# Attention decode: keys and values of both batch entries in one load of 32 KB rows, exponentials by batch entry

## The chip, the cores and the metric

One core of a Trainium2 chip. The metric is the device time of one execution in microseconds (us), without a profile for the comparison and with one for the traces. A kernel's time is the median of its runs; a verdict rests on ratios with a 95% interval. The batches of experiments ran on different chips, on which the kernel before took 190.50 to 190.68 us; times are therefore compared within a batch or by their ratios.

## The reference

One decode step: a layer norm of x (2 batch entries, 448 features), grouped-query attention with 16 query heads on 8 key/value heads over the last 4,096 cache positions, a dense layer with a Mish activation beside it, and the sum of x and both.

```python
W = min(4096, max(256, Sk // 4))                     # 4096 positions
q = (xn @ wq) -> (B, 16 heads, 256)
k = k_cache[:, :, Sk - W:, :]; v = v_cache[:, :, Sk - W:, :]   # 2 x 8 x 4096 x 256, bf16
p = softmax(q . k * 256 ** -0.5); o = p . v
out = x + o @ wo + (h * tanh(softplus(h))) @ w2      # h = xn @ w1 + b1
```

K and V are 67.1 MB of the 77.7 MB that one execution reads.

## The kernel before

It goes through 16 pairs of (key/value head, batch entry). Each pair's 4,096 keys lie as 128 partitions x 32 rows x 256 numbers, so that a partition's load is one run of 16 KB.

```python
heads = [(kvh, b) for kvh in range(Hkv) for b in range(Bsz)]
def load_k(i):                       # k_pool: 4 buffers of 16 KB a partition; V: 5
    kvh, b = heads[i]
    t = k_pool.tile([P, T * Dh], BF16, tag="k", name="k")
    nc.sync.dma_start(out=t[:],
        in_=A_k_cache[b, kvh, s0:Sk, :].rearrange("(p t) d -> p (t d)", p=P))
...
def turn(s):      nc.vector.transpose(kt, k half)        # 128 x 2048 words, L364
def scores(s):    8 matmuls of 512 columns into psc       # L376
                  nc.scalar.activation(out=p_sb, in_=psc, func=Exp, accum_out=rs)   # L386
def turn_p(s):    nc.vector.transpose(pT, p_sb)           # L397
def values(i):    16 matmuls of 512 columns, then 4 output transposes    # 12 of the pairs
def values_fixed(i):  64 matmuls of 2 columns, no transposes after it    # the last 4 pairs
def mix(kvh):     16 matmuls of 112 columns: oT @ wo into psA
...
for i in range(NK + KA):             # loads run two pairs ahead of the scores
    load_k(i + 2); load_v(i, cuts); load_wo(kvh)          # all on one DMA queue, in this order
    for half in range(NH): turn(s + 1); scores(s); turn_p(s - 1); close(i - KA - 1)
    build_q(i + 2); values(i - KA)
```

The last V load is cut into 1 MB, 0.5 MB and 0.5 MB, and the last weights come after it.

The softmax here doesn't subtract the row's maximum and nothing guards it: scores larger than these inputs give would overflow.

## Time and profile before

| | before |
|---|---|
| time, median of 3 | 190.59 us (190.53 to 190.59) |
| span of the profiled run | 188.7 us |
| packets of the big DMA queue, MB | 7,796, 77.66 |
| mean rate over the span | 413 GB/s, 428 to 431 in the middle |
| busy: TensorE, VectorE, ScalarE | 76%, 60%, 17% |

A busy share says little here; what counts is that the row of DMA digits has no hole. The lines are in the prediction below.

### The profile page before, as it was taken

The numbers are of one execution on the slowest core, as the hardware profiler recorded it, in microseconds if no ns is written. First come the engines' busy times: TensorE is split into PE (matmuls) and PEld (weight loads), VectorE is DVE, ScalarE is ACT, GpSimd is POOL, SyncE is SP. The second block draws the span as 40 slices with busy tenths as digits, with TensorE's granted clock in tenths as the row PEclk, the third lists the DMA queues.
The fourth block names the chain that finished last, engine by engine and source line by source line (L and its number), as shares of the span: only waits on it lengthen the run. The fifth ranks groups of instructions, "written<-read, shape, count | busy, mean of one in ns | idle before, by whom it ended". The sixth has DMA issues, their size and how long they took to land.

```text
span 188.7 us, 2944 instructions
## 1 busy us (share of the span) xinstructions
PE 144.1 (76%) x1158; PEld 71.7 (38%) x1158; DVE 113.5 (60%) x195; ACT 32.5 (17%) x82; POOL 27.1 (14%) x139
## 2 busy tenths in 40 slices
PE   0152991788995799869985999769986999597782
PEld 0042390234442345334432434324533443254671
DVE  7805505997919392857649381939376673939401
ACT  2300110112212022111222112202311121211101
POOL 8004430033030022003030203003110300000000
PEclk9999995799999699988999699969998799969955
DMA  6999999999999999999999999999999999999991
GB/s 216 423 432 422 430 430 434 438 431 420 417 441 431 420 416 438 441 427 405 442 434 429 434 420 431 434 431 420 431 431 438 412 432 434 431 441 417 408 394 49
DMA packets 7816, 77.86 MB, mean 413 GB/s; under 512 B 757, under 2 KB 2809, under 8 KB 3322
## 3 DMA queue, kind: packets, MB, share of 16 engines
q1 hardware_dynamic: 7796, 77.66, 97.3%
q8 instruction: 9, 0.15, 0.3%
q14 instruction: 5, 0.04, 0.1%
q10 hardware_dynamic: 6, 0.01, 0.0%
HBM read 77.67 MB, written 0.00 MB: 412 GB/s over the span
## 4 chain that ended last, share of the span: by engine, by line
DMA 82%; DVE 11%; issue 2%; PE 2%; SPq 1%; ACT 0%; ACTq 0%
DMA k<-in_A_k_cache_dram 68%; DMA v<-in_A_v_cache_dram 14%; DVE kt L364 8%; DVE pT L397 2%; PE sc L376 1%; SPq L114 0%; PE psA L214 0%; SPq L338 0%; PE q L479 0%; SPq L280 0%; DVE sums L407 0%; SPq L275 0%; DVE sums L404 0%; DVE den_sb L320 0%; ACT p L386 0%
## 5 line engine op out<-in xcount | busy, mean ns | idle before, releaser
L364 DVE STREAM_TRANSPOSE kt<-k 128x2048 f32<-128x2048 f32 x32 | 73.4, 2296 | 50.6 <-DMA k<-in_A_k_cache_dram 49.6
L376 PE MATMUL sc<-kt,qdiag 128*128 128x512 bf16 x256 | 72.7, 433 | 17.6 <-DVE kt L364 15.8
L376 PEld LDWEIGHTS <-qdiag 128*128 128x128 bf16 x256 | 24.7, 105 | 57.2 <-issue 30.0
L431 PE MATMUL o<-v,pT 128*4 128x512 bf16 x192 | 43.4, 379 | 0.0
L264 POOL COPY qdiag<-qrep 32x8 bf16<-32x8 bf16 x128 | 23.1, 213 | 122.4 <-PE sc L376 107.6
L386 ACT ACTIVATE p<-sc 128x512 bf16<-128x512 f32 x32 | 19.1, 597 | 95.6 <-PE sc L376 93.1
L431 PEld LDWEIGHTS <-pT 128*4 128x4 bf16 x192 | 15.8, 87 | 21.8
L397 DVE STREAM_TRANSPOSE pT<-p 128x512 bf16<-128x512 bf16 x32 | 21.5, 672 | 1.1 <-ACT p L386 1.1
L439 ACT COPY o_sb<-o 4x512 f32<-4x512 f32 x12 | 6.9, 574 | 36.8 <-PE o L431 36.8
L214 PE MATMUL psA<-wo,oT 128*2 128x112 bf16 x128 | 3.8, 245 | 11.0 <-DVE oT L447 11.0
L479 PE MATMUL q<-pT,v 128*128 128x2 bf16 x256 | 7.6, 165 | 1.7 <-DMA v<-in_A_v_cache_dram 1.6
L460 PEld LDWEIGHTS q<-ident_f,o_sb 4*128 4x128 f32 x48 | 6.6, 206 | 5.1 <-issue 5.1
L479 PEld LDWEIGHTS <-v 128*128 128x128 bf16 x256 | 7.3, 101 | 2.0 <-DMA v<-in_A_v_cache_dram 2.0
L414 PEld LDWEIGHTS den<-sums,ones_f 128*128 128x128 f32 x32 | 6.8, 220 | 3.3 <-issue 1.7
L460 PE MATMUL q<-ident_f,o_sb 4*128 4x4 f32 x48 | 7.6, 261 | 0.0
L235 PE MATMUL qT_ps<-xs,v 128*128 128x4 bf16 x112 | 3.3, 166 | 4.8 <-DVE ones L201 2.8
L214 PEld LDWEIGHTS <-oT 128*2 128x2 bf16 x128 | 1.8, 87 | 11.9 <-DVE oT L447 11.7
L386 ACT ACTIVATION_READ_ACCUMULATOR p<-sc 128x1 f32 x32 | 6.2, 194 | 0.0
L177 PE MATMUL xnT_ps<-ident,xn_bf 2*128 2x2 bf16 x7 | 0.5, 167 | 6.3 <-DVE xn_bf L139 6.3
L414 PE MATMUL den<-sums,ones_f 128*128 128x2 f32 x32 | 5.1, 229 | 0.0
L235 PEld LDWEIGHTS <-v 128*128 128x128 bf16 x112 | 3.1, 104 | 5.0 <-issue 3.0
L462 DVE COPY osum<-q 128x4 f32<-128x4 f32 x12 | 1.9, 158 | 3.9 <-PE q L460 3.9
(52 smaller groups left out, 46.5 us busy)
## 6 DMA issues: line engine op xcount, KB each, us to landing
k<-in_A_k_cache_dram SPq DMA_DIRECT2D x16, 2048.0 KB, 31.5
v<-in_A_v_cache_dram SPq DMA_DIRECT2D x15, 2048.0 KB, 34.8
v<-in_B_w_dram SPq DMA_DIRECT2D x2, 1568.0 KB, 21.0
wo<-in_A_wo_dram SPq DMA_DIRECT2D x7, 448.0 KB, 31.5
v<-in_A_wq_dram SPq DMA_DIRECT2D x1, 2048.0 KB
v<-in_A_wq_dram SPq DMA_DIRECT2D x1, 1536.0 KB, 10.8
v<-in_A_v_cache_dram SPq DMA_DIRECT2D x1, 1024.0 KB, 29.1
v<-in_A_v_cache_dram SPq DMA_DIRECT2D x2, 512.0 KB, 27.4
```

What stands on the lines that cost most here:

```text
L214: nc.tensor.matmul(part(n), lhsT=lhsT, rhs=w[:, n * DO : (n + 1) * DO], start=start, stop=stop, tile_position=(0, n * Q), skip_group_check ...
L235: nc.tensor.matmul(qT_ps[:, hh, e, :], lhsT=wq_v[s][:, hh, e, :], rhs=xs[:, s, :, :].rearrange("p x b -> p (x b)"), start=(s == 0), stop=( ...
L264: nc.gpsimd.tensor_copy(out=tv[rows, :, e, j * Q : (j + 1) * Q : HS], in_=qrep[rows, :, h0 : h0 + rep, e, x, b],)
L364: nc.vector.transpose(out=kt[:].bitcast(FP32), in_=k[:, half * TH * Dh : (half + 1) * TH * Dh].bitcast(FP32),)
L376: nc.tensor.matmul(psc[:], lhsT=qdiag[i % NW][:, n * NE + e, :], rhs=ktv[:, n, e, :, :], start=(n == 0 and e == 0), stop=(n == NB - 1 and ...
L386: nc.scalar.activation(out=p_sb[:], in_=psc[:].rearrange("p t c -> p (t c)"), func=ACT.Exp, scale=scale, accum_out=state["rs", i][:, s % N ...
L397: nc.vector.transpose(out=pT[:], in_=p_t.pop(s)[:])
L414: nc.tensor.matmul(den[:], lhsT=ones_f[:], rhs=state.pop(("sums", i))[:], start=True, stop=True)
L431: nc.tensor.matmul(po[:], lhsT=pT_t[i * NH + half][:, uh * NP * Q : (uh + 1) * NP * Q : HS], rhs=v[:, u * NP : (u + 1) * NP, :].rearrange( ...
L439: nc.scalar.copy(out=o_sb[:], in_=po[:])
L460: nc.tensor.transpose(pqv[:, u, c, :], ov[:, u, c, :], ident_f[0:NR, 0:NR])
L479: nc.tensor.matmul(po[:, c, :], lhsT=vv[:, t, c, :], rhs=pTv[:, th, 0:Q:HS], start=(t == 0 and c == 0), stop=(t == T - 1), skip_group_chec ...
```

## The change

The intent: read both batch entries of a head at once, so that loads are 4 MB and rows 32 KB, and halve the number of loads, denominators and output transposes. Partition 2p + b holds row p of entry b. A score row belongs to one entry, so the exponentials of the other entry's partitions must vanish: two exponentials over every second column, with a bias of 0 on the rows of their own entry and -10,000 on the others.

```diff
-    T = W // P
-    NH = 2
+    PB = P // Bsz
+    T = W // PB
+    TH = 16
+    NH = T // TH
...
-    k_pool = ... bufs=4
-    v_pool = ... bufs=5
+    k_pool = ... bufs=2          # of twice the size
+    v_pool = ... bufs=2
...
+    def load_cache(t, cache, i, cuts):
+        src = cache[:, i, s0:Sk, :].rearrange("b (p t) d -> p b (t d)", p=PB)
+        for lo, hi in zip(cuts, cuts[1:]):
+            cols = slice(lo * Dh, hi * Dh)
+            nc.sync.dma_start(out=t[:, cols], in_=src[:, :, cols])
...
-        nc.scalar.activation(out=p_sb[:], in_=psc[:]..., func=ACT.Exp, scale=scale, accum_out=...)
+        for b in range(Bsz):
+            nc.scalar.activation(out=pv[:, b, :, :], in_=sv[:, b, :, :], func=ACT.Exp,
+                scale=scale, bias=off[:, b : b + 1], accum_out=...)
...
-            load_v(i, (0, T) if i < NK - 1 else (0, T // 2, 3 * T // 4, T))
+            load_v(i, (0, T) if i < Hkv - 1 else (0, T // 2, 7 * T // 8, T))
...                                # query building, output transposes and sums by head, not by pair
```

The last V load is now cut into 2 MB, 1.5 MB and 0.5 MB.

More of the change, by code (lines that the diff above doesn't have):

```diff
@@ L61 @@
     F = B_w1.shape[1]
-    T = W // P
-    NH = 2
-    TH = T // NH
+    PB = P // Bsz
+    T = W // PB
+    TH = 16
+    NH = T // TH
+    BR = Bsz * rep
     NX = 2
@@ L73 @@
     NE = 2
-    HS = Q // rep
+    HS = Q // BR
     assert Sq == 1 and D * NX == NS * P and NS % 2 == 1 and HF % P == 0 and Hq % NX == 0
@@ L83 @@
     wo_pool = ctx.enter_context(tc.tile_pool(name="wo", bufs=3))
-    k_pool = ctx.enter_context(tc.tile_pool(name="kk", bufs=4))
-    v_pool = ctx.enter_context(tc.tile_pool(name="vv", bufs=5))
-    kt_pool = ctx.enter_context(tc.tile_pool(name="kt", bufs=3))
+    k_pool = ctx.enter_context(tc.tile_pool(name="kk", bufs=2))
+    v_pool = ctx.enter_context(tc.tile_pool(name="vv", bufs=2))
+    kt_pool = ctx.enter_context(tc.tile_pool(name="kt", bufs=4))
     consts = ctx.enter_context(tc.tile_pool(name="consts", bufs=1))
@@ L100, with v_tile @@
     nc.scalar.dma_start(out=b1_sb[:, :], in_=B_b1.rearrange("(o f) -> o f", o=1))
-    def v_tile(n):
-        t = v_pool.tile([P, T * Dh], BF16, tag="v", name="v")
-        return t[:, 0:n]
-    SC = NS // 2 + 1
-    wq_in = A_wq.rearrange("r (x n) -> (r x) n", x=NX).rearrange("(p s) n -> p s n", s=NS)
-    wq_sb = []
-    for lo, hi in ((0, SC), (SC, NS)):
-        w = v_tile((hi - lo) * HW).rearrange("p (s n) -> p s n", n=HW)
-        nc.sync.dma_start(out=w, in_=wq_in[:, lo:hi, :])
-        wq_sb += [w[:, s, :] for s in range(hi - lo)]
+    def v_tile():
+        return v_pool.tile([P, T * Dh], BF16, tag="v", name="v")
+    wq_sb = v_tile()[:, 0 : NS * HW].rearrange("p (s n) -> p s n", s=NS)
+    nc.sync.dma_start(
+        out=wq_sb,
+        in_=A_wq.rearrange("r (x n) -> (r x) n", x=NX).rearrange("(p s) n -> p s n", s=NS),
+    )
     make_identity(nc, ident[:])
@@ L158 @@
             )
-    hsel = hsel[:, 0:rep]
+    hsel = hsel[:, 0:BR]
     nc.vector.tensor_copy(out=hsel, in_=ident[:, 0:Q:HS])
@@ L164 @@
         )
+    off = consts.tile([P, Bsz], FP32)
+    for b in range(Bsz):
+        nc.vector.tensor_reduce(
+            out=off[:, b : b + 1], in_=hsel[:, b * rep : (b + 1) * rep], axis=AXIS.X, op=ALU.add
+        )
+    mine = consts.tile([P, 1], FP32)
+    nc.vector.tensor_reduce(out=mine[:], in_=hsel, axis=AXIS.X, op=ALU.add)
+    nc.vector.tensor_scalar(
+        out=off[:], in0=off[:], scalar1=mine[:], scalar2=1e4, op0=ALU.subtract, op1=ALU.mult
+    )
     ones_f = consts.tile([P, P], FP32)
     nc.gpsimd.memset(ones_f[:], 1.0)
-    NW = 3
+    NW = 2
     qdiag = []
@@ L227 @@
     qrep = consts.tile([P, NB, HH, NE, NX, Bsz], BF16)
-    wq_v = [w.rearrange("p (h m e) -> p h e m", h=HH, e=NE) for w in wq_sb]
+    wq_v = wq_sb.rearrange("p s (h m e) -> p s h e m", h=HH, e=NE)
     def project():
@@ L236, in project @@
                         qT_ps[:, hh, e, :],
-                        lhsT=wq_v[s][:, hh, e, :],
+                        lhsT=wq_v[:, s, hh, e, :],
                         rhs=xs[:, s, :, :].rearrange("p x b -> p (x b)"),
@@ L252, in project @@
         )
-    heads = [(kvh, b) for kvh in range(Hkv) for b in range(Bsz)]
     def build_q(i):
-        kvh, b = heads[i]
-        x, h0 = divmod(kvh * rep, HH)
+        x, h0 = divmod(i * rep, HH)
         t = qdiag[i % NW]
@@ L264, in build_q @@
                 nc.gpsimd.tensor_copy(
-                    out=tv[rows, :, e, j * Q : (j + 1) * Q : HS],
-                    in_=qrep[rows, :, h0 : h0 + rep, e, x, b],
+                    out=tv[rows, :, e, j * Q : (j + 1) * Q : HS].rearrange(
+                        "p n (b h) -> p n b h", b=Bsz
+                    ),
+                    in_=qrep[rows, :, h0 : h0 + rep, e, x, :].rearrange("p n h b -> p n b h"),
                 )
@@ L273, in load_dense @@
     def load_dense():
-        dense["w1"] = v_tile(NS * HF).rearrange("p (s n) -> p s n", s=NS)
+        w = v_tile()
+        dense["w1"] = w[:, 0 : NS * HF].rearrange("p (s n) -> p s n", s=NS)
         nc.sync.dma_start(
@@ L278, in load_dense @@
         )
-        dense["w2"] = v_tile(NX * NF * D).rearrange("p (x c d) -> p x c d", x=NX, c=NF)
+        dense["w2"] = w[:, NS * HF : NS * HF + NX * NF * D].rearrange(
+            "p (x c d) -> p x c d", x=NX, c=NF
+        )
         nc.sync.dma_start(
@@ L328, in dense_out, with load_k @@
                 add(act_bf[:, c, x, :], w2_sb[:, x, c, :])
-    NSTEP = len(heads) * NH
+    NSTEP = Hkv * NH
     k_t, kt_t, v_t, p_t, pT_t, wo_t = {}, {}, {}, {}, {}, {}
     state = {}
-    def load_k(i):
-        kvh, b = heads[i]
-        t = k_pool.tile([P, T * Dh], BF16, tag="k", name="k")
-        nc.sync.dma_start(
-            out=t[:], in_=A_k_cache[b, kvh, s0:Sk, :].rearrange("(p t) d -> p (t d)", p=P)
-        )
-        k_t[i] = t
-    def load_v(i, cuts=(0, T)):
-        kvh, b = heads[i]
-        t = v_tile(T * Dh).rearrange("p (t d) -> p t d", t=T)
-        vin = A_v_cache[b, kvh, s0:Sk, :].rearrange("(p t) d -> p t d", p=P)
-        for lo, hi in zip(cuts, cuts[1:]):
-            nc.sync.dma_start(out=t[:, lo:hi, :], in_=vin[:, lo:hi, :])
-        v_t[i] = t
+    def load_cache(t, cache, i, cuts):
[3 more added lines that the diff above has]
+            nc.sync.dma_start(out=t[:, cols], in_=src[:, :, cols])
+    def load_k(i, cuts=(0, T)):
+        k_t[i] = k_pool.tile([P, T * Dh], BF16, tag="k", name="k")
+        load_cache(k_t[i], A_k_cache, i, cuts)
+    def load_v(i, cuts=(0, T)):
+        t = v_tile()
+        load_cache(t, A_v_cache, i, cuts)
+        v_t[i] = t[:].rearrange("p (t d) -> p t d", t=T)
     def load_wo(kvh, parts=1):
@@ L383, in scores @@
         p_sb = p_pool.tile([P, TH * Q], BF16, tag="p", name="p")
-        if s % NH == 0:
-            state["rs", i] = small.tile([P, NH], FP32, tag="rs", name="rs")
-        nc.scalar.activation(
-            out=p_sb[:],
-            in_=psc[:].rearrange("p t c -> p (t c)"),
-            func=ACT.Exp,
-            scale=scale,
-            accum_out=state["rs", i][:, s % NH : s % NH + 1],
-        )
+        piece = s % NH
+        if piece == 0:
+            state["rs", i] = small.tile([P, NH, Bsz], FP32, tag="rs", name="rs")
+        pv = p_sb[:].rearrange("p (t c b) -> p b t c", t=TH, b=Bsz)
+        sv = psc[:].rearrange("p t (c b) -> p b t c", b=Bsz)
+        for b in range(Bsz):
+            nc.scalar.activation(
+                out=pv[:, b, :, :],
+                in_=sv[:, b, :, :],
+                func=ACT.Exp,
+                scale=scale,
+                bias=off[:, b : b + 1],
+                accum_out=state["rs", i][:, piece, b : b + 1],
+            )
         p_t[s] = p_sb
     def turn_p(s):
-        pT = p_pool.tile([P, TH * Q], BF16, tag="pT", name="pT", bufs=7)
+        pT = p_pool.tile([P, TH * Q], BF16, tag="pT", name="pT", bufs=2 * NH + 1)
         nc.vector.transpose(out=pT[:], in_=p_t.pop(s)[:])
@@ L402, in turn_p @@
         rs = state.pop(("rs", i))
-        sums = small.tile([P, rep], FP32, tag="sums", name="sums", bufs=4)
+        total = small.tile([P, 1], FP32, tag="total", name="total")
+        nc.vector.tensor_reduce(out=total[:], in_=rs[:], axis=AXIS.XY, op=ALU.add)
+        sums = small.tile([P, BR], FP32, tag="sums", name="sums")
         nc.vector.tensor_scalar(
-            out=sums[:], in0=hsel, scalar1=rs[:, 0:1], scalar2=None, op0=ALU.mult
-        )
-        nc.vector.scalar_tensor_tensor(
-            out=sums[:], in0=hsel, scalar=rs[:, 1:2], in1=sums[:], op0=ALU.mult, op1=ALU.add
+            out=sums[:], in0=hsel, scalar1=total[:], scalar2=None, op0=ALU.mult
         )
@@ L412, in denominator @@
     def denominator(i):
-        den = ps_m.tile([P, rep], FP32, tag="m", name="den")
+        den = ps_m.tile([P, BR], FP32, tag="m", name="den")
         nc.tensor.matmul(
@@ L416, in denominator @@
         )
-        rec = small.tile([P, rep], FP32, tag="rec", name="rec")
+        rec = small.tile([P, BR], FP32, tag="rec", name="rec")
         nc.vector.reciprocal(out=rec[:], in_=den[:])
@@ L421 @@
     NP = 2
-    NR = NP * rep
+    NR = NP * BR
     def values(i):
@@ L429, in values @@
         for u in range(T // NP):
-            half, uh = divmod(u, TH // NP)
+            piece, uh = divmod(u, TH // NP)
             nc.tensor.matmul(
                 po[:],
-                lhsT=pT_t[i * NH + half][:, uh * NP * Q : (uh + 1) * NP * Q : HS],
+                lhsT=pT_t[i * NH + piece][:, uh * NP * Q : (uh + 1) * NP * Q : HS],
                 rhs=v[:, u * NP : (u + 1) * NP, :].rearrange("p t d -> p (t d)"),
@@ L442, in scale_o @@
     def scale_o(i, o):
-        kvh, b = heads[i]
         rec = state.pop(("rec", i))
-        if b == 0:
-            state["oT"] = small.tile([P, ND, rep, Bsz], BF16, tag="oT", name="oT")
+        oT = small.tile([P, ND, rep, Bsz], BF16, tag="oT", name="oT")
         nc.vector.tensor_tensor(
-            out=state["oT"][:, :, :, b],
-            in0=o,
-            in1=rec[:].unsqueeze(1).to_broadcast([P, ND, rep]),
+            out=oT[:].rearrange("p c h b -> p c b h"),
+            in0=o.rearrange("p c (b h) -> p c b h", b=Bsz),
+            in1=rec[:]
+            .rearrange("p (b h) -> p b h", b=Bsz)
+            .unsqueeze(1)
+            .to_broadcast([P, ND, Bsz, rep]),
             op=ALU.mult,
         )
+        state["oT", i] = oT
     def finish(i):
@@ L460, in finish @@
                 nc.tensor.transpose(pqv[:, u, c, :], ov[:, u, c, :], ident_f[0:NR, 0:NR])
-        o = small.tile([P, ND, rep], FP32, tag="osum", name="osum")
-        nc.vector.tensor_copy(out=o[:], in_=pqv[:, 0, :, 0:rep])
+        o = small.tile([P, ND, BR], FP32, tag="osum", name="osum")
+        nc.vector.tensor_copy(out=o[:], in_=pqv[:, 0, :, 0:BR])
         for u in range(1, NP):
             nc.vector.tensor_tensor(
-                out=o[:], in0=o[:], in1=pqv[:, u, :, u * rep : (u + 1) * rep], op=ALU.add
+                out=o[:], in0=o[:], in1=pqv[:, u, :, u * BR : (u + 1) * BR], op=ALU.add
             )
-        scale_o(i, o[:])
+        scale_o(i, o)
     def values_fixed(i):
@@ L472, in values_fixed @@
         pq = ps_q.tile([P, NP * ND * NR], FP32, tag="q", name="q")
-        po = pq[:, 0 : ND * rep].rearrange("p (c h) -> p c h", c=ND)
+        po = pq[:, 0 : ND * BR].rearrange("p (c h) -> p c h", c=ND)
         vv = v_t.pop(i).rearrange("p t (m c) -> p t c m", c=ND)
         for t in range(T):
-            half, th = divmod(t, TH)
-            pTv = pT_t[i * NH + half][:].rearrange("p (t c) -> p t c", t=TH)
+            piece, th = divmod(t, TH)
+            pTv = pT_t[i * NH + piece][:].rearrange("p (t c) -> p t c", t=TH)
             for c in range(ND):
@@ L489, in mix @@
     def mix(kvh):
-        oT = state["oT"]
+        oT = state.pop(("oT", kvh))
         w = wo_t.pop(kvh)
@@ L498, in mix, with close @@
                 )
-    NK = len(heads)
-    KA = 2
+    NFIX = 2
+    def close(i):
+        if i < Hkv - NFIX:
+            finish(i)
+        mix(i)
     load_k(0)
     load_dense()
-    load_k(1)
     project()
@@ L509 @@
     turn(0)
-    NFIX = 4
-    def close(i):
-        if i < NK - NFIX:
-            finish(i)
-        kvh, b = heads[i]
-        if b == Bsz - 1:
-            mix(kvh)
-    for i in range(NK + KA):
-        if i + 2 < NK:
-            load_k(i + 2)
-        if i < NK:
-            load_v(i, (0, T) if i < NK - 1 else (0, T // 2, 3 * T // 4, T))
-            kvh, b = heads[i]
-            if b == Bsz - 1:
-                load_wo(kvh, parts=1 if i < NK - 1 else 2)
-            for half in range(NH):
-                s = i * NH + half
+    for i in range(Hkv + 1):
+        if i + 1 < Hkv:
+            load_k(i + 1, (0, T) if i + 1 < Hkv - 1 else (0, T // 2, T))
+        if i < Hkv:
+            load_v(i, (0, T) if i < Hkv - 1 else (0, T // 2, 7 * T // 8, T))
+            load_wo(i, parts=1 if i < Hkv - 1 else 2)
+            for piece in range(NH):
+                s = i * NH + piece
                 if s + 1 < NSTEP:
@@ L535 @@
                     turn_p(s)
-                if half == 0 and i > KA:
-                    close(i - KA - 1)
-            if i + 2 < NK:
+                if piece == 0 and i > 1:
+                    close(i - 2)
+            if i + 2 < Hkv:
                 build_q(i + 2)
-        if i == NK:
-            close(i - KA - 1)
+        else:
+            close(i - 2)
         if i == 0:
             dense_in()
-        if i == 1:
             dense_out()
-        if i >= KA:
-            if i - KA < NK - NFIX:
-                values(i - KA)
-            else:
-                values_fixed(i - KA)
-        if i >= NK:
-            close(i - KA)
+        if i >= 1:
+            if i - 1 < Hkv - NFIX:
+                values(i - 1)
+            else:
+                values_fixed(i - 1)
+        if i == Hkv:
+            close(i - 1)
     res = consts.tile([Bsz, D], BF16)
```

## The prediction

The forecast is 190.59 - 1.0 = 189.6 us: 0.9 us for packets and 0.14 us for completions, both from packet times in the trace of the kernel before, and 0 for all else. The completions are the 754 packets of 4 bytes in the trace of the kernel before, 16 for each of 47 loads and 2 more, with a median of 9 ns.

> **What bounds the kernel now.** I read the page from its slices to its chain of waits, then the windows view, the groups and the timeline of the end. The slices come first, because they tell whether one resource is busy throughout:
>
> ```profile
> PE   0152991788995799869985999769986999597782
> DVE  7805505997919392857649381939376673939401
> PEclk9999995799999699988999699969998799969955
> DMA  6999999999999999999999999999999999999991
> GB/s 216 423 432 422 430 430 434 438 431 420 417 441 431 420 416 438 441 427 405 442 434 429 434 420 431 434 431 420 431 431 438 412 432 434 431 441 417 408 394 49
> ```
>
> The reader is to see that the DMA row is 9 from the second slice to the last but one, while PE and DVE come and go. The kernel streams 77.66 MB and computes in the shadow of it. The chain of waits and the queue table say the same in shares:
>
> ```profile
> q1 hardware_dynamic: 7796, 77.66, 97.3%
> ...
> DMA 82%; DVE 11%; issue 2%; PE 2%; SPq 1%; ACT 0%; ACTq 0%
> DMA k<-in_A_k_cache_dram 68%; DMA v<-in_A_v_cache_dram 14%; DVE kt L364 8%; DVE pT L397 2%; PE sc L376 1%; SPq L114 0%; PE psA L214 0%; SPq L338 0%; PE q L479 0%; SPq L280 0%; DVE sums L407 0%; SPq L275 0%; DVE sums L404 0%; DVE den_sb L320
> ```
>
> Packets of the one big queue fill 97.3% of 16 engines for the whole span: 183.6 of 188.7 us. The DVE share of the chain is no second bound: a buffer's release is one of the events before an issue, but the queue in front of that issue is still full, as the windows show (us, busy of PE, weight load, DVE, ACT, POOL, then clock, DMA share, GB/s):
>
> ```profile
> 40.00:60.00 20.00, 17.23 (x80) 7.38 (x80) 14.76 (x20) 3.90 (x10) 3.45 (x20) 1.00 1.01 428
> ...
> 120.00:140.00 20.00, 17.89 (x92) 7.82 (x92) 12.53 (x20) 3.61 (x10) 2.91 (x16) 0.91 1.01 431
> ```
>
> DMA share is 1.01 in every middle window. What remains outside the stream is the start (the first packet starts at 1.7 us) and the end: the last V packets end at 183.9 us, the last value matmuls run from 184.31, the output is issued at 186.51, and the span ends at 188.7. That is 1.7 + 4.8 us around a stream of 182 us. The groups I need for costs:
>
> ```profile
> L364 DVE STREAM_TRANSPOSE kt<-k 128x2048 f32<-128x2048 f32 x32 | 73.4, 2296 | 50.6 <-DMA k<-in_A_k_cache_dram 49.6
> L376 PE MATMUL sc<-kt,qdiag 128*128 128x512 bf16 x256 | 72.7, 433 | 17.6 <-DVE kt L364 15.8
> L431 PE MATMUL o<-v,pT 128*4 128x512 bf16 x192 | 43.4, 379 | 0.0
> L386 ACT ACTIVATE p<-sc 128x512 bf16<-128x512 f32 x32 | 19.1, 597 | 95.6 <-PE sc L376 93.1
> L397 DVE STREAM_TRANSPOSE pT<-p 128x512 bf16<-128x512 bf16 x32 | 21.5, 672 | 1.1 <-ACT p L386 1.1
> L386 ACT ACTIVATION_READ_ACCUMULATOR p<-sc 128x1 f32 x32 | 6.2, 194 | 0.0
> ```
>
> DVE's idle time (49.6 us) is mostly a wait for K to land: the engines wait for the data, not the data for them.
>
> [...] Built, the new load reads a pattern of 64 x 2 x 16384 elements into 128 partitions[...]. No load of the kernel before has unequal outer sizes, so its trace shows nothing of this. [...]
>
> **The change part by part.**
> *Loads.* Sixteen K loads and as many V heads of 2 MB become eight of 4 MB each, with rows of 32 KB where there were 16 KB. The bytes are the same. In the packet records of the trace, grouped by size, a packet is one row: medians are 74 ns for 1,792 bytes, 159 for 4,096, 309 for 8,192, 460 for 12,288 and 611 for 16,384. From 8,192 to 16,384 bytes, (611 - 309)/8192 = 0.0369 ns a byte, and 309 - 302 = 7 ns that do not scale. So I estimate 1,215 ns for a 32 KB packet, against 2 x 611. Count: before, 31 whole loads and 3 pieces of 128 rows are 4,352 packets; after, 14 whole loads, 2 pieces of K and 3 of V are 19 x 128 = 2,432. The query weights, now one load, save another 128. Saved: 2,048 packets x 7 ns / 16 engines = 0.9 us. Each load also writes one completion of 9 ns an engine: 48 loads of that queue become 32, 16 x 9 ns = 0.14 us. All on the path, since the stream is the bound: **-1.0 us**.
> *TensorE and VectorE.* Counted in the built programs: scores stay 256 matmuls of 512 columns, values 192 of 512 and 256 small ones (4 columns for 2), transposes 32 + 32. Denominators go from 16 to 8, output transposes from 48 to 24, and their small VectorE operations halve: together they are busy for 15.2 us now, so some 7.6 us go, all of it beside the stream: **0**.
> *ScalarE.* 32 exponentials of 512 become 64 of 256 with a pointer bias. [...] PT is needed only a head later: **0**.
> *GpSimd.* 128 query copies become 64 of twice the width, in the shadow: **0**.
> *Buffers.* K has 2 of 32 KB a partition instead of 4 of 16, V 2 instead of 5 halves. A head is now 4.19 + 4.19 + 0.46 MB, at 430 GB/s 9.8 + 9.8 + 1.05 = 20.6 us. Take K(i) landed at 0. Its four transposes with four of P between them last 4 x (2.30 + 0.67) = 11.9 us, then its buffer is free. The transfer that needs it, K(i+2), starts after V(i-1), weights, K(i+1), V(i), weights: at 31.4 us. Slack 19 us. V(i-1) is free after the scores (about 14 us) and 32 value matmuls of 43.4/192 = 0.226 us, 7.2 us: at 21 us; V(i+1) starts at 41 us. Even with scores at the slow clock (the timeline has one group of 8 in 3.32 us instead of 1.90), 13 us are left. **0**.
> *Start.* The second buffer of V first holds both dense weights, and V(1) must wait for the dense product, which VectorE does behind the transpose of K(1). K(1) lands near 15.3 MB / 0.43 = 36 + 2 us; the product is done near 45 us; V(1)'s turn in the queue is near 57. **0**.
> *End.* The last V piece is 512 KB as before (8 of 64 rows a partition for 8 of 32), followed by the same weights, 16 value matmuls and 16 matmuls of the output: **0**, with 0.3 us either way.
>
> Sum: 190.59 - 1.0 = 189.6 us.
>
> **Rivals.** *A, the deal of rows to engines or the two distant entries slow the stream.* Neighbouring rows now lie 128 MiB apart in HBM[...]. For it: nothing in the trace has this pattern. Against it: [...] each row is long, and the order within partitions is plain. A mild form (1 to 2% lower rate) gives 191 to 193 us[...]. I give the two together 10%. *B, two coarse buffers open gaps in the stream.* For it: PE is busy 17 to 18 of every 20 us, so a head needs nearly its whole period, and arrivals are lumpier. Against: the slack of 13 to 20 us above. One gap of 2 us at the start would make 191.5; one a head would make over 200. I give 5%. *C, the longer rows buy more than 7 ns.* [...] 5%.
>
> **Range and chances.** The mechanism gives -1.0 with an uncertainty of some 0.7 for the fit of the 7 ns and the end. A mild form of A or B stretches the range upwards. Range 188.6 to 191.3. Faster by over 2% (under 186.8) needs C and more: 0.04. Slower by over 2% (over 194.4) needs A or B in full: 0.09. Within 2%: 0.87.
>
> **What would show it right or wrong.** Right: the DMA row stays at 9, about 5,490 packets in the big queue (7,796 - 2,048 - 256), packets of 32 KB near 1,215 ns, middle windows at 431 to 434 GB/s[...], the last load to the end unchanged at 4 to 5 us. Wrong: 32 KB packets over 1,230 ns or GB/s below 425 with the DMA row at 9 speak for A; a digit under 9 in the middle of the DMA row, with the queue waiting for a transpose or a value matmul, speaks for B; GB/s over 435 for C.

## The result

| | before | after |
|---|---|---|
| median of 4 runs each | 190.56 us (190.51 to 190.59) | 190.46 us (190.30 to 190.64) |
| ratio of the means | | 0.9995, interval 0.9978 to 1.0013 |

Ratios are the mean time of one kernel's fast runs over that of the other's from the same rounds, so they are not quite the ratio of the medians quoted. The time lies inside the predicted range, but the forecast gain of 1.0 us did not come: 0.1 us did, no more than noise, and a repetition (below) had 0.0.

The page of the changed kernel, the lines that answer to those shown of before (DMA share and rate in 40 slices, queues, chain of waits):

```profile
DMA  6999899999999999999999999999999999999990
GB/s 226 445 444 428 383 432 438 445 442 440 431 431 438 445 407 404 433 438 398 462 447 431 431 431 438 414 418 420 449 431 431 412 423 435 473 418 386 427 375 23
...
q1 hardware_dynamic: 5492, 77.66, 96.8%
q8 instruction: 8, 0.13, 0.2%
...
DMA 67%; DVE 18%; PE 11%; ACT 1%; SPq 0%; issue 0%; ACTq 0%; DVEq 0%
```

The packets fell by 2,304, as counted. Queue q8, of kind "instruction", moves packets of 16 KB (8 of them, 0.13 MB), called fetches below. They seem to be TensorE's: the runs with 11 matmuls alone, stream32 and stream16, have none, and 1,152 more TensorE instructions (more_instr) come with four more, 12 for 8. One digit in the early part is an 8. It is no gap: the packet records show at least 16 packets in flight at every moment from 12 to 172 us, read here as all 16 engines busy, and the run with loads alone (below) has the same 8. Two of the six middle windows, and the groups of the exponentials (all six, from 40 to 160 us, run at 422 to 435 GB/s, 429.7 on average, against 428.7 before):

```profile
40.00:60.00 20.00, 14.91 (x115) 6.97 (x116) 12.62 (x16) 4.52 (x17) 1.64 (x8) 0.81 1.02 435
...
120.00:140.00 20.00, 16.52 (x83) 6.87 (x81) 12.15 (x14) 4.87 (x17) 1.64 (x8) 0.83 1.00 428
```

```profile
L403 ACT ACTIVATE p<-sc,off 128x256 bf16<-128x256 f32 x64 | 33.0, 544 | 84.2 <-PE sc L389 83.5
...
L403 ACT ACTIVATION_READ_ACCUMULATOR p<-sc,off 128x1 f32 x64 | 11.7, 183 | 0.0
```

ScalarE's share rose from 17% to 22%, in the shadow. What the DMA queue's issues waited for (total us, times, longest), before and then after:

```profile
SPq L348 <- DMA k<-in_A_k_cache_dram: 31.3, 7, 4.5
```

```profile
SPq L353 <- PE o L448: 55.0, 6, 11.4
SPq L353 <- DVE kt L377: 54.3, 6, 10.3
```

The new kernel's issues do wait for value matmuls and transposes, 109 us in all, because it has two buffers. Yet the stream has no hole: a K load is issued a median of 29.7 us before it lands, so these waits are inside the slack. The rival of coarse buffers is out.

**The last microseconds** differ. The windows of 1 us (same columns as above; the last two are DMA share and GB/s), before:

```profile
182.00:183.00 1.00, 0.88 (x32) 0.79 (x30) 0.00 (x0) 0.00 (x0) 0.00 (x0) 0.50 1.00 406
183.00:184.00 1.00, 0.59 (x16) 0.51 (x16) 0.00 (x0) 0.00 (x0) 0.00 (x0) 0.50 0.89 350
184.00:185.00 1.00, 0.59 (x16) 0.50 (x16) 0.07 (x1) 0.00 (x0) 0.00 (x0) 0.50 0.59 219
```

and after:

```profile
182.00:183.00 1.00, 0.25 (x9) 0.25 (x10) 0.00 (x0) 0.00 (x0) 0.00 (x0) 0.50 0.93 360
183.00:184.00 1.00, 1.00 (x43) 1.00 (x41) 0.00 (x0) 0.00 (x0) 0.00 (x0) 0.50 0.55 213
184.00:185.00 1.00, 0.74 (x29) 0.63 (x25) 0.17 (x1) 0.00 (x0) 0.00 (x0) 0.50 0.12 43
```

From 183 us on, most engines of the new kernel have nothing left (share 0.55, then 0.12, against 0.89 and 0.59). The trace records 16 landings for the last V piece, taken here as one for each of the 16 DMA engines: the first at 182.55 and the last at 184.27 us before, at 181.79 and 183.95 after. Before, the matmuls that read the piece begin at 184.31, just after the last. Most engines are done earlier by most of the gain that was forecast, but some work on: the first engine gained 0.76 us, the last 0.32.

The timeline after that piece (start, us, engine, line, work, idle before it and its releaser), before:

```profile
184.31 0.59 PE L479 MATMUL q<-pT,v 128*128 128x2 bf16 x16 [0.63 <-DMA v<-in_A_v_cache_dram]
184.94 0.17 DVE L447 TENSOR_TENSOR oT<-q,rec 128x4 bf16<-128x4 f32 x1 [3.00 <-PE q L479]
185.16 0.68 PE L214 MATMUL psA<-wo,oT 128*2 128x112 bf16 x16 [0.26 <-DVE oT L447]
...
186.51 0.34 SPq L558 DMA_DIRECT2D out_dram<-res  x1
```

and after:

```profile
182.75 1.87 PE L498 MATMUL q<-pT,v 128*128 128x4 bf16 x64 [1.52 <-DMA v<-in_A_v_cache_dram]
184.66 0.17 DVE L462 TENSOR_TENSOR oT<-q,rec 128x8 bf16<-128x8 f32 x1 [5.59 <-PE q L498]
184.88 0.70 PE L225 MATMUL psA<-wo,oT 128*2 128x112 bf16 x16 [0.26 <-DVE oT L462]
...
186.19 0.33 SPq L568 DMA_DIRECT2D out_dram<-res  x1
```

The reader is to see that the new kernel's last 48 + 16 value matmuls run as one group, since the piece before the last is 1.5 MB. The run tailcut, below, cuts it finer.

### The profile page after: what moved, and what is told of

Same layout as the page of the kernel before. It is cut to its first block, busy times and chain, and to the rows that moved or that the text cites. A ratio compares the mean times of both kernels' runs of the same rounds, so it can differ in the third digit from the quotient of the medians.

```text
span 188.4 us, 2773 instructions
## 1 busy us (share of the span) xinstructions
PE 138.5 (74%) x1118; PEld 68.2 (36%) x1118; DVE 106.0 (56%) x155; ACT 41.4 (22%) x140; POOL 16.1 (9%) x74
## 3 DMA queue, kind: packets, MB, share of 16 engines
q1 hardware_dynamic: 5492, 77.66, 96.8%
## 4 chain that ended last, share of the span: by engine, by line
DMA 67%; DVE 18%; PE 11%; ACT 1%; SPq 0%; issue 0%; ACTq 0%; DVEq 0%
DMA k<-in_A_k_cache_dram 58%; DVE kt L377 14%; DMA v<-in_A_v_cache_dram 10%; PE sc L389 6%; PE o L448 4%; DVE pT L415 3%; PE q L498 1%; PE psA L225 1%; ACT p L403 1%; DVE oT L462 0%; DVE sums L424 0%; SPq L353 0%; DVE osum L483 0%; SPq L111 0%; ACTq L595 0%
## 5 line engine op out<-in xcount | busy, mean ns | idle before, releaser
L403 ACT ACTIVATE p<-sc,off 128x256 bf16<-128x256 f32 x64 | 33.0, 544 | 84.2 <-PE sc L389 83.5
L448 PE MATMUL o<-v,pT 128*8 128x512 bf16 x192 | 42.5, 379 | 0.0
L448 PEld LDWEIGHTS <-pT 128*8 128x8 bf16 x192 | 17.2, 92 | 22.4
L272 POOL COPY qdiag<-qrep 32x16 bf16<-32x16 bf16 x64 | 13.0, 247 | 121.8 <-PE sc L389 107.4
L403 ACT ACTIVATION_READ_ACCUMULATOR p<-sc,off 128x1 f32 x64 | 11.7, 183 | 0.0
L456 ACT COPY o_sb<-o 8x512 f32<-8x512 f32 x6 | 3.4, 574 | 36.3 <-PE o L448 36.3
L498 PE MATMUL q<-pT,v 128*128 128x4 bf16 x256 | 7.4, 168 | 1.9 <-DMA v<-in_A_v_cache_dram 1.8
L479 PEld LDWEIGHTS q<-ident_f,o_sb 8*128 8x128 f32 x24 | 3.3, 206 | 3.0 <-issue 3.0
L479 PE MATMUL q<-ident_f,o_sb 8*128 8x8 f32 x24 | 3.8, 264 | 0.0
L303 PE MATMUL hT_ps<-xs,v 128*128 128x4 bf16 x49 | 3.7, 195 | 0.0
## 6 DMA issues: line engine op xcount, KB each, us to landing
k<-in_A_k_cache_dram SPq DMA_DIRECT2D x7, 4096.0 KB, 29.7
wo<-in_A_wo_dram SPq DMA_DIRECT2D x7, 448.0 KB, 29.7
```

The source lines that it names most:

```text
L272: nc.gpsimd.tensor_copy(out=tv[rows, :, e, j * Q : (j + 1) * Q : HS].rearrange("p n (b h) -> p n b h", b=Bsz), in_=qrep[rows, :, h0 : h0 + ...
L303: nc.tensor.matmul(hT_ps[:, c, :, :].rearrange("p x b -> p (x b)"), lhsT=w1_v[:, s, c, :], rhs=xs[:, s, :, :].rearrange("p x b -> p (x b)" ...
L403: nc.scalar.activation(out=pv[:, b, :, :], in_=sv[:, b, :, :], func=ACT.Exp, scale=scale, bias=off[:, b : b + 1], accum_out=state["rs", i] ...
L448: nc.tensor.matmul(po[:], lhsT=pT_t[i * NH + piece][:, uh * NP * Q : (uh + 1) * NP * Q : HS], rhs=v[:, u * NP : (u + 1) * NP, :].rearrange ...
L456: nc.scalar.copy(out=o_sb[:], in_=po[:])
L479: nc.tensor.transpose(pqv[:, u, c, :], ov[:, u, c, :], ident_f[0:NR, 0:NR])
```

## The experiments

All runs are timed against the kernel before in the same rounds, four to six runs each. One table holds what the traces gave. "Mean engine" is the time that packets cover, those of the fetches included (about 0.5 us an engine with 8 fetches): the number of packets in flight, at most 16, summed from the first load's start (1.7 to 1.8 us) to the last load's end and divided by 16. "First" and "last" are the engines landing the last V piece. "Fetches" are the 16 KB packets on the instruction queue that begin before the last engine has landed that piece; three or four fetches of 8 KB on another queue, in all runs but those of loads alone, are not counted.

| run | median us | ratio (95%) | mean engine us | first, last us | spread us | fetches |
|---|---|---|---|---|---|---|
| before | 190.56 | 1 | 182.52 | 182.55, 184.27 | 1.72 | 8 |
| again_before | 190.57 | 0.9998 (0.9986, 1.0011) | 182.66 | 182.46, 184.33 | 1.87 | 8 |
| after | 190.46 | 0.9995 (0.9978, 1.0013) | 181.75 | 181.79, 183.95 | 2.15 | 8 |
| again_after | 190.69 | 1.0000 (0.9988, 1.0013) | 181.73 | 181.85, 183.85 | 2.00 | 8 |
| rows16 | 190.76 | 1.0010 (0.9997, 1.0024) | 182.44 | 182.42, 184.66 | 2.24 | 8 |
| rows8 | 191.80 | 1.0064 (1.0051, 1.0077) | 183.90 | 183.95, 186.10 | 2.15 | 8 |
| stream32 | 188.08 | 0.9869 (0.9855, 0.9882) | 180.91 | 181.72, 182.54 | 0.82 | 0 |
| stream16 | 188.62 | 0.9895 (0.9882, 0.9909) | 181.54 | 182.40, 183.03 | 0.63 | 0 |
| more_instr | 191.73 | 1.0065 (1.0051, 1.0079) | 182.19 | 181.73, 185.46 | 3.72 | 12 |
| more_work | 189.92 | 0.9984 (0.9966, 1.0002) | 181.75 | 181.75, 183.80 | 2.05 | 8 |
| nfix1 | 192.44 | 1.0098 (1.0084, 1.0112) | 181.57 | 181.63, 183.89 | 2.26 | 7 |
| fewer_instr | 190.87 | 1.0017 (1.0005, 1.0029) | 181.65 | 181.58, 183.88 | 2.30 | 7 |
| fewer_tail | 190.78 | 1.0003 (0.9990, 1.0015) | 181.70 | 181.79, 183.84 | 2.05 | 7 |
| shift14 | 190.75 | 1.0006 (0.9994, 1.0018) | 181.66 | 181.95, 183.86 | 1.91 | 8 |
| shift63 | 190.24 | 0.9990 (0.9965, 1.0014) | 181.96 | 181.85, 184.50 | 2.65 | 9 |
| tailcut | 190.46 | 0.9988 (0.9975, 1.0001) | 181.75 | 181.74, 184.00 | 2.26 | 8 |
| shift63_tail | 190.15 | 0.9978 (0.9966, 0.9989) | 181.81 | 181.84, 183.82 | 1.98 | 8 |
| before_shift63 | 191.70 | 1.0053 (1.0039, 1.0066) | 182.65 | 182.44, 185.45 | 3.02 | 9 |

### Do longer rows save anything? again_after, again_before, rows16, rows8

Theory 1: the saving is real, but the last of 16 engines sets the end. Theory 2: in a full stream long rows save nothing. The first two are the kernels unchanged. rows16 cuts every whole load in two and leaves the pieces of the last K and V. rows8 cuts into pieces of at most 1 MB, the last K and V too, so that its last V piece but one is 0.5 MB as well.

```diff
+        cuts = sorted(set(cuts) | set(range(0, T, 32)))     # rows16; 16 for rows8
         for lo, hi in zip(cuts, cuts[1:]):
```

> The changed kernel once more, for the spread of its times and a second trace. Theory 1 (uneven engines): the longer rows do save about 0.8 us of the mean engine's packet time, but the end is set by the one of 16 DMA engines that is furthest behind, and where instruction fetches of 16 KB fall differs from run to run; so times scatter by 0.2 us or more about 190.4 and the spread between the first and the last engine to land the last V piece (1.72 us before, 2.15 us after in the first traces) comes out different again, by 0.3 us or more. Theory 2 (rows of 32 KB save nothing at all in a full stream): the times equal those of the kernel before within 0.1 us, whatever the spread.

> The kernel before against itself: ratio 1.000 within 0.001, the noise of this comparison. A second trace: theory 1 expects the spread of the engines at the last V piece to be 1.5 to 2.2 us again, and the mean busy time of the stream to be 0.6 to 0.9 us longer than in the changed kernel's traces.

> The changed kernel with every whole K and V load cut in two, so that a row is 16 KB again and all else stays: 1,792 packets and 14 loads more. Theory 1: the mean engine needs 0.6 to 0.9 us more; the time rises to about 191.1, less or more by 0.4 us as the engines' spread falls out. Theory 2: 190.4 as the changed kernel, within 0.2.

> The changed kernel with loads cut in four, rows of 8 KB: 5,888 packets more than the changed kernel and 46 loads more. With 5 to 7 ns a packet over 16 engines and 9 ns a load and engine, theory 1 expects 2.2 to 3.0 us more: 192.6 to 193.4. Theory 2: within 0.3 us of 190.4.

Measured: the mean engine of both traces of the changed kernel is 0.8 to 0.9 us shorter than in both of the kernel before (181.74 against 182.59 on average). Cutting the rows in two gives 0.70 us back, in four 2.16 us. So theory 2 is out: 2.16 us x 16 engines / 5,888 packets = 5.9 ns a packet, completions of the extra loads included. In the time, less of it shows: rows8 is slower by 1.1 to 1.3 us than the two medians of the changed kernel, below the 2.2 expected, and rows16 only by 0.1 to 0.3: its 190.76 us is inside the expected band (190.7 to 191.5) at the low edge. Something in the end part gives time back to the cut versions. And the spread of the engines in again_after is 0.15 us off the first trace, less than the 0.3 expected: it seems to belong to the kernel more than to the run, as far as two traces of each can tell. By its time alone the repetition fits theory 2 (190.69 against 190.65 us for the kernel before in its rounds); only the mean engine and rows8 refute it. The A/A comparison shows the noise, 0.1%.

### The disputed cost by itself: stream32, stream16

The loads of each kernel, in order and size, without work on them.

```diff
-    project(); build_q(...); turn(0); ... all scores, values and sums
+    res = last V piece + last weights          # waits for both to land
```

> All loads of the changed kernel in their order and sizes, with no work on them but one sum of the last V piece and the last weights (a wrong result on purpose): the disputed cost by itself. TensorE has almost no instructions, so hardly any instruction fetch disturbs the 16 engines. Theory 1: the engines end within 1 us of one another at the last V piece, and this run is shorter than the one with the loads of the kernel before by 0.6 to 1.0 us. Theory 2: no difference beyond 0.2 us.

> All loads of the kernel before (16 KB rows, 47 loads), with no work on them but the same sum at the end (a wrong result on purpose). Theory 1: engines within 1 us of one another at the last V piece, 0.6 to 1.0 us longer than the run with the changed kernel's loads. Theory 2: the same within 0.2 us.

The last windows, first with the rows of 32 KB, then with those of 16 KB:

```profile
182.00:183.00 1.00, 0.00 (x0) 0.00 (x0) 0.00 (x0) 0.00 (x0) 0.00 (x0) 1.00 0.83 314
183.00:184.00 1.00, 0.00 (x0) 0.00 (x0) 0.35 (x1) 0.00 (x0) 0.00 (x0) 1.00 0.05 18
```

```profile
182.00:183.00 1.00, 0.00 (x0) 0.00 (x0) 0.00 (x0) 0.00 (x0) 0.00 (x0) 1.00 1.01 393
183.00:184.00 1.00, 0.00 (x0) 0.00 (x0) 0.00 (x0) 0.00 (x0) 0.00 (x0) 1.00 0.52 197
```

Without work the engines end within 0.6 to 0.8 us of each other, and the longer rows win 0.54 us of the time (188.62 - 188.08) and 0.63 us of the mean engine. The first is just under the expected 0.6 to 1.0, the second at its low end. Load by load, stream32 keeps a spread of 0.75 to 0.82 us from 12 us to the end, stream16 one of 0.62 to 0.70 (wherever the landings of a load can be told from those of its neighbours): with loads alone the engines do not drift apart. Here there is no instruction fetch at all.

### Fetches or work? more_instr, more_work, nfix1

more_instr adds 576 tiny matmuls, which need instructions but little time; more_work adds 64 large ones, busy for about as long (20.0 against 19.0 us), with a ninth of the instructions. 8 fetches for the 2,190 instructions are about 274 instructions each, an estimate. nfix1 takes 184 instructions away (its expectation says 188).

```diff
                 scores(s)
+                idle_matmuls(18)          # more_instr: 18 matmuls of 2 columns, never read
...
+        for _ in range(2):                # more_work: the first score matmul, twice for nothing
+            nc.tensor.matmul(psc[:], lhsT=qdiag[i % NW][:, 0, :], rhs=ktv[:, 0, 0, :, :], start=True, stop=True)
...
-    NFIX = 2
+    NFIX = 1                              # nfix1
```

> The changed kernel with 576 unused matmuls of 2 columns (18 after each of the 32 groups of scores), 1,152 more TensorE instructions with their weight loads, [...] from 2,190 instructions against 8 fetches of 16 KB: 4 to 5 fetches more. TensorE gets about 2 us of work a head, in the shadow. Theory 1: no gap in the middle of the DMA row, 12 or 13 fetches instead of 8, the mean engine 0.2 to 0.3 us longer, and the slowest engine 0.2 to 1.1 us later: 190.7 to 191.5. Theory 2 (fetches do not matter, or TensorE has room): 190.4 within 0.2.

> The changed kernel with the seventh head's values by the form with 512 columns (one head instead of two in the form of single blocks): 188 TensorE instructions fewer, so one fetch less or none. Theory 1: 190.0 to 190.5, the outcome again hanging on which engines the fetches meet. Theory 2: the same as the changed kernel within 0.1 us.

> Control for the run with 576 idle matmuls: the changed kernel with the first matmul of each group of scores done three times instead of once (the first two are overwritten, the result stays right). TensorE gets about as much time more (64 matmuls of 512 columns, 0.43 to 0.85 us a group against about 0.5) but only 128 instructions more, half a fetch of 16 KB. Theory 1 (fetches put single DMA engines behind): 8 or 9 fetches, spread at the last V piece 2.0 to 2.3 us as in the changed kernel, time within 0.3 us of it, 190.3 to 190.9. Rival (TensorE's time itself delays the end): about 191.7, as the run with idle matmuls.

more_instr's output was wrong, which was not intended. Its loads, work and instruction counts are as described, so its times stand. Its last windows:

```profile
183.00:184.00 1.00, 0.30 (x12) 0.21 (x8) 0.00 (x0) 0.00 (x0) 0.00 (x0) 0.50 0.51 196
184.00:185.00 1.00, 0.72 (x26) 0.72 (x27) 0.00 (x0) 0.00 (x0) 0.00 (x0) 0.50 0.29 114
185.00:186.00 1.00, 1.00 (x43) 1.00 (x41) 0.00 (x0) 0.00 (x0) 0.00 (x0) 0.50 0.28 97
```

About a quarter of the engines work alone for two microseconds: four land the last V piece 3.2 to 3.7 us after the first. With 12 fetches in place of 8 the first engine lands when it did (181.73), the last 1.5 us later, and the time rises by 1.0 to 1.3 us, to more than the expected 190.7 to 191.5. With more_work the spread stays at 2.05 us. As a control it is not perfect, for TensorE's whole busy time rose by 3.6 us there and by 10.0 us in more_instr. The landings of the single loads are the better evidence: the spread jumps where a fetch falls and then stays. In more_instr it goes from 1.06 to 2.61 us across the fetch begun at 17.85 us, and from 2.33 to 3.87 across the one at 141.37. In the first trace of before it goes from 0.56 to 1.74 us across the fetch at 17.07 (1.2 us, though that packet itself took 0.97) and ends at 1.72. In the first trace of after it rises across three fetches, the first of them from 0.76 to 1.57 us at 18.25, and ends at 2.15; in again_after it goes from 0.74 to 2.27 across the first, at 17.71, and ends at 2.00. Most other fetches in these traces change it by 0.2 us or less. The fetch near 17 us falls where the work on the first K begins, so that at 141.37, and one at 183.31 in before_shift63 below, weigh more. So in these traces it is instruction fetches, not TensorE's time, that put single DMA engines behind, by 0.8 to 1.6 us at each of these jumps.

more_work was also a surprise: 189.92 us, 0.6 us under the kernel before, with as much spread as the changed kernel (four of its six runs lie between 189.84 and 189.93, two at 190.5 and 191.1). It was meant as a control, but its 128 extra TensorE instructions also shift the program, as the shifts below do on purpose: its last 16 matmuls take 0.54 us without a standstill, where the changed kernel's two traces have 0.70 and 1.17. nfix1 missed for a simple reason: the seventh head's values now hold TensorE until 181 us, and the eighth head's start long after their data:

```profile
183.57 3.56 PE L498 MATMUL q<-pT,v 128*128 128x4 bf16 x128
```

Its time tells nothing of fetches; its one fetch fewer (7) left the spread at 2.26 us.

### A version with fewer instructions: fewer_instr, fewer_tail

```diff
+    psB: a second sum, x + dense + six heads by one matmul of 448 columns instead of four of 112
+    add(ident, psB as bf16, start=True)   # joins the last two heads
...
-            load_v(i, ... (0, T // 2, 7 * T // 8, T))
+            load_v(i, ... (0, T // 2, 3 * T // 4, 7 * T // 8, T))     # fewer_tail only
```

> The changed kernel with 226 TensorE instructions fewer: x, the dense part and six of eight heads are summed by one matmul of 448 columns where four of 112 stood, in a PSUM bank of its own, and that sum joins the last two heads at the end. [...] one instruction fetch fewer (7 for 8). Theory 1: mean engine about 0.06 us shorter, the slowest engine between unchanged and 1.1 us earlier, depending on which engine is spared: 189.5 to 190.6. Rival (the rest of the end part decides, not the fetches): as the changed kernel, 190.4 to 190.7, with the same spread.

> The same with fewer TensorE instructions, and the last V piece but one (1.5 MB) cut into 1 MB and 0.5 MB, so that TensorE isn't still at 48 value matmuls when the last piece lands. Theory 1 expects at most 0.1 us from the cut: in the timeline the last 16 value matmuls start when the piece lands and end 0.6 us later, instead of 0.7 us. Time 189.4 to 190.5; a candidate to beat both kernels.

Both missed. One fetch fewer left the spread as it was (2.30 and 2.05 us), so the number alone does not set it; presumably it is which engines the fetches meet, but the records do not name engines. And both were slower than expected, because TensorE stood still shortly before the end of its work, for 0.62 and 1.00 us. That standstill led to the next theory. The repetition of the changed kernel has one as well, among its last 16 matmuls:

```profile
184.82 0.35 PE L225 MATMUL psA<-wo,oT 128*2 128x112 bf16 x5 [0.26 <-DVE oT L462]
...
185.54 0.45 PE L225 MATMUL psA<-wo,oT 128*2 128x112 bf16 x11 [0.37 <-issue]
```

"issue" is idle time for which the profile shows no waited-for event. The weights had landed at 185.18 us, so it was not them. Counting TensorE's records (matmuls and weight loads) from the start, the standstill is after number 2,214 in both traces of the changed kernel, and after 1,958 = 2,214 - 256 in fewer_instr and fewer_tail; and it ends 2.3 to 2.4 us after an instruction fetch began, in all four.

### Does the place of the last fetch decide? shift14, shift63, tailcut, shift63_tail

Theory 1b, the inference from these places: TensorE reaches instructions whose fetch is late. If so, a few instructions at the very start, where TensorE is idle (in the changed kernel its first matmul starts at 5.10 us, and from 6.06 to 12.09 us it waits again), move the place.

```diff
-    for s in range(NS):
+    for s in [s for _ in range(3) for s in range(NS)]:     # shift14; range(10) for shift63
         nc.tensor.transpose(xnT_ps[:, s, :], ...)
...
-            load_v(i, ... (0, T // 2, 7 * T // 8, T))
+            load_v(i, ... (0, T // 2, 3 * T // 4, 7 * T // 8, T))     # tailcut, shift63_tail
```

> The changed kernel with 14 repeated small transposes of x at the very start (28 TensorE instructions, no work later). In the traces so far TensorE stands still, waiting for nothing shown, at the instruction with the same number counted from the start (2,214) and only 2.3 to 2.4 us after an instruction fetch began: 22 instructions before the end in both traces of the changed kernel (0.2 and 0.37 us), 52 before the end in both with fewer instructions (0.6 and 1.0 us), exactly 256 [...] apart from 1,958. Theory 1b (a late fetch holds TensorE in the final stretch, and where depends on the instruction count): with 28 more the place moves to 50 before the end, among the last 16 value matmuls; a standstill of 0.5 to 1.0 us there, time 190.7 to 191.2. Rival (chance, or the end part as such): as the changed kernel, 190.4 to 190.7, no standstill there.

> The same with 63 repeated transposes at the start (126 instructions, under 4 us of TensorE's idle start). Theory 1b: the place moves to 148 before the end, where TensorE waits for V anyway; no standstill after the last V piece, time 189.8 to 190.1, so about -0.6 us of the kernel before, with the spread of the engines still 1.9 to 2.3 us. Rival: 190.4 to 190.7.

> The changed kernel with only the last 1.5 MB piece but one of V cut into 1 MB and 0.5 MB. Theory 1b: TensorE goes on with the second half of the values about 1.2 us earlier, so the last fetch starts about 1.2 us earlier (near 181.5 instead of 182.8) and has landed before it is needed: no standstill, 189.9 to 190.2. Rival: gains at most the 0.1 us of the shorter last group, 190.3 to 190.6.

> Both: 63 repeated transposes at the start and the finer cut at the end; the candidate to beat both kernels. Theory 1b: no standstill in the final stretch, 189.8 to 190.1, hardly better than either alone.

shift14 did what was said. Its 190.75 us, hardly above the rival's band (to 190.7), would not decide; the place does. The standstill sits 50 records before the end, among the last value matmuls, again after number 2,214:

```profile
182.69 1.63 PE L498 MATMUL q<-pT,v 128*128 128x4 bf16 x55 [1.17 <-DMA v<-in_A_v_cache_dram]
...
184.87 0.41 PE L498 MATMUL q<-pT,v 128*128 128x4 bf16 x9 [0.55 <-issue]
```

The fetch began at 182.56 us, 2.3 us before TensorE went on. In shift63 that standstill is gone, and the median is 190.24 us, 0.1 us above the expected band; its runs scatter from 189.86 to 191.75, and in its profiled run (190.63) one engine was 2.65 us behind. tailcut missed, and its rival came: the last fetch began at 183.06 us, not at 181.5, a standstill of 0.17 us remained, and the time was 190.46 us. So the finer cut alone does not bring the fetch forward. Both edits together, shift63_tail, have no standstill in the values and give 190.15 us, just above the expected band, ratio 0.9978 with an interval that ends at 0.9989: the only complete version here whose interval lies below 1, by 0.2%. It has the lowest ratio of ten variants that were tried, so even this is weak.

### Is it the shift or the rows? before_shift63

The same 63 transposes in the kernel before.

```diff
-    for s in range(NS):
+    for s in [s for _ in range(10) for s in range(NS)]:
```

> Control: the kernel before with the same 63 repeated transposes at the start. Its own traces show no standstill of TensorE after the last V piece (the place of the last fetch, instruction 2,214, is 102 before its end, where it waits for V). Theory 1b (the gain of the shifted changed kernel is the longer rows' 0.4 to 0.8 us at the slowest and the mean engine, set free): the kernel before gains nothing, ratio 0.999 to 1.002. Rival (the repeated transposes help by themselves): 190.1 to 190.3, as the shifted changed kernel.

Neither: it became slower by 1.0 us. The timeline shows where:

```profile
183.09 0.58 PE L479 MATMUL q<-pT,v 128*128 128x2 bf16 x16 [0.21 <-DMA v<-in_A_v_cache_dram]
...
185.50 0.59 PE L479 MATMUL q<-pT,v 128*128 128x2 bf16 x16 [1.82 <-DMA v<-in_A_v_cache_dram]
```

TensorE waits 1.82 us for the last V piece, where it waited 0.63. The slowest engine was 1.86 us behind at the piece before, 3.02 us at the last; the second slowest stayed at 1.83. An instruction fetch had begun at 183.31 us, between the two, on the engine that then ended last (inferred from the landings). So moving instructions by 126 places costs this kernel 1.0 us: the repetition does not help by itself, and what it does depends on where the fetches fall. Between the two shifted kernels, 190.2 and 191.7 us, lie 1.5 us, more than the rows can explain.

## Why the prediction was wrong, by its steps

- **What bounds the kernel.** Right: the stream has no hole before or after, until the last 2 us.
- **Packets.** The count was exact: 5,492, as 7,796 - 2,048 - 256. A 32 KB packet took 1,213 ns, against 1,215 estimated. The saving was oversized a little: -1.04 us estimated, -0.85 us measured in the mean engine (182.59 to 181.74, two traces each), -0.63 us with loads alone. The step took the part of a packet's duration that does not scale (7 ns) for engine time, but packets overlap: in the first traces the durations on the big queue add up to 183.7 us an engine before and 182.4 after, and cover 182.0 and 181.2. The direct measurement (rows8) is 5.9 ns a packet with completions, where the estimate comes to 8.1.
- **"All on the path, since the stream is the bound": the step that failed.** The end waits for the slowest of 16 engines, and then for TensorE's last instructions. The spread between first and last engine was 1.72 and 1.87 us before, 2.15 and 2.00 us after, so of 0.68 us gained by the first engine (averages: 182.51 to 181.82) 0.40 us reached the last (184.30 to 183.90). The prediction took the end of the last V packets, 183.9 us, for the end of the stream; the trace it had showed a first engine at 182.55 and a last at 184.27, and it did not ask whether a saving reaches the last one in full. The runs show what feeds the spread: without TensorE's instructions it is 0.63 to 0.82 us, with four more fetches 3.72 us, with more TensorE time alone 2.05 us, and it jumps at single fetches. Why the changed kernel's eight fetches leave 0.3 us more than the eight before is not shown.
- **"End: 0, with 0.3 us either way."** Here a term was missing: whether TensorE can run through its last instructions. From the landing of the last V piece to the end of the span the kernel before takes 4.45 and 4.40 us, the changed kernel 4.41 and 4.88. The difference lies in the second trace alone, in its last 16 matmuls: 1.17 us with a standstill of 0.37, against 0.70 in the first trace and 0.68 and 0.63 before. rows16 and rows8, with the last fetch begun at 181.9 and 180.8 us instead of 182.8 or later, take 4.1 us and so lost less time than their engines did. Part of that is the missing standstill (16 matmuls in 0.59 us); 0.16 us of it lies after the output has landed, and no record shows why. What sets the start of the last fetch stays open: with the 1.5 MB piece of V cut finer (tailcut) it began no earlier.
- **The sum.** -0.85 in the mean engine, -0.40 at the slowest, +0.2 on average in the end part leaves about -0.2 us in the span. The medians say -0.10 and, in the repetition, +0.04. That last 0.1 to 0.2 us is within the scatter of single runs (the trace of the repetition is its slowest run, 190.84 us) and stays unexplained.
- **Engines and ScalarE.** Beside the stream, as foreseen. The exponentials of 256 columns took 544 ns, and 0.73 us with their read of 183 ns, against 597 and 194 ns for 512 columns before; ScalarE was busy for 22% of the span, against 17%.
- **Rivals.** A is out: the middle of the stream runs at 429.7 GB/s against 428.7, and all 16 engines work on the 64 x 2 pattern (at least 16 packets in flight at every moment from 12 to 172 us). One window of 20 us had 422, under the 425 that was to speak for A; but the next had 435, and the mean engine was faster than before. The mean rate stayed under the 431 to 434 foreseen. B is out: issues wait 109 us for buffers, none of it reaches the stream. C did not come: a 32 KB packet took 1,213 ns, against 1,215 estimated, and the middle ran at 429.7 GB/s.

What stays open: which engine a fetch meets, and so why one layout of instructions ends with 1.7 and another with 3.0 us of spread; and the link from a late fetch to a standstill is inferred from its place (2,214 or 1,958) and its delay (2.3 to 2.4 us), and supported by shift14, where the place moved as foreseen, not by a record that names the fetch as the releaser.

## What to carry to other kernels

In this kernel, bound by a load stream, a saving of engine time counted at the slowest of the 16 engines: of 0.68 us at the first, 0.40 us reached the last. So compare the first and the last landing of the final load before and after, not the mean rate. When a change moves under 1% of the time, test it with a few instructions shifted at the start: here 126 harmless ones moved the kernel before by +1.0 us, more than the change under study. A standstill that no event explains may be a late instruction fetch (here 0.2 to 1.0 us, ending 2.3 to 2.4 us after a fetch began, and inferred, not recorded): count the instructions up to it in several versions, and look for a fetch begun shortly before. A finer cut of the final load, which was to bring that fetch forward, was not shown to help (tailcut, 190.46 us).
